# A branch flag one step earlier, a hint for the branch, and the arms in the other order

## The chip, the cores and the metric

The kernel runs on one core of one Trainium2 chip. The metric is the device time in microseconds (us) of one execution. Before the change three runs took 209.24, 209.59 and 210.6 us, median 209.59 us. One more execution was recorded with the hardware profiler; all durations below come from it unless another source is named.

## The reference

The reference mixes two blocks of a model over a sequence of 2048 tokens of width 512, in bfloat16:

```
g = sigmoid((x * gate_w).sum(-1, keepdims=True))
a: q, k, v = x @ wqkv, 32 heads of 16;  pq = q @ w_phi, pk = k @ w_phi (per head)
   phi = concat(softmax(p), softmax(-p)) for p = pq and p = pk
   kv = phi_k^T v;  z = sum of phi_k;  o = (phi_q kv) / (phi_q z + 1e-6);  a = o @ wo
b: z = gelu(x @ w_in) in two halves z1, z2;  z2 = layernorm(z2)
   b = (z1 * (w_sp @ z2 + b_sp)) @ w_out
out = g * a + (1 - g) * b
```

The softmax needs care. `exp` without the row maximum taken off is fast, and it is right as long as no sum of exponentials grows too large. The kernel computes that fast form, keeps watch over the sums, and holds a second, slower form (with the maximum) ready in the same program. A flag computed on the chip decides which of the two delivers the output. With the inputs of the reference the fast form is the one that is used.

## The kernel before

The tokens are cut into 16 tiles of 128 (NT = 16). The first stage computes `z`, the gate and the projections of all tiles. The second computes the keys' features and the products with `w_sp`, in halves of 344 columns (`gg_half`, 32 of them). The last stage is the loop `for j in range(NT)`. Its step j multiplies the queries' features with `kvx` (`q_mm`, L471), divides and gates on VectorE (`q_num`, L477 and L479), transposes `o` into `oT` by a DMA that SyncE issues (L486), and, three steps later, multiplies the finished tile into the output (`out_tile`, L492 and L497; L506 copies the result out of PSUM on ScalarE and L507 starts its DMA). So step 14 runs `out_tile(11)`, step 15 runs `out_tile(12)`, and three output tiles, 13, 14 and 15, are left when the loop ends.

The program is written under a manual schedule: each engine executes its instructions in the order in which the Python code issues them. TensorE (PE in the profile) has the longest list by far, 2746 instructions up to the branch, and its sequencer dispatches them into a queue ahead of their execution.

The flag comes about as follows. GpSimd (POOL) adds up in `worst` all sums and their reciprocals. In step 13 `check_sums` (L455, L456, VectorE, DVE in the profile) turns them into a column of ones and zeros, `safeb`, and `count_safe` (L461) lets TensorE add up that column, into one number in PSUM bank 0: it is 128 if all partitions are safe. In step 14 `copy_count` (L466) copies the number to `flag`. After the loop `nc.values_load` (L614) makes each of the five engines read `flag` into a register of its own. `out_mm` of tile 13 follows, and then the branch (L617): `tc.If(safe < P)`. The first arm is the general form, 1105 TensorE instructions and 319 on VectorE. The `Else` arm is what is executed here. It has 62 TensorE instructions, the copy of tile 13 and all of tiles 14 and 15. In the program's memory the general arm stands right behind the branch and the fast arm behind the general one, so each engine has to jump over the general arm.

```
        if j == NT - 2:
            copy_count()
    safe = nc.values_load(flag[0:1, 0:1], min_val=0, max_val=P)
    out_mm(NT - 3, 5)
```

Tile 15 is split into 384 and 128 columns. The copy of the last 128 columns (L506) and its DMA (L507), both on ScalarE, are the last work of the kernel; the end of the program waits for that DMA.

Of the kernel before, what the change touches and what calls it, by code (L numbers as in the profile page):

```python
# [8 lines left out]
ALU = mybir.AluOpType  # L9
# [5 lines left out]
P = 128  # L15
S = 2048
D = 512
# [5 lines left out]
NT = S // P  # L23
# [17 lines left out]
def kernel(  # L41
# [14 lines left out]
    nc = tc.nc  # L56
# [9 lines left out]
    ps = psp.tile([P, 8, CH], FP32, name="ps")  # L66

    def zbank(t):
# [29 lines left out]
    flag = pers.tile([1, 1], I32, name="flag")  # L98
# [9 lines left out]
        out=ident[:], in_=ident[:], pattern=[[-1, P]],  # L108
# [14 lines left out]
    for d0 in (0, 2):  # L123
# [6 lines left out]
        out=wv[:, :, :],  # L130
        in_=A_wqkv[:, 2 * D:3 * D].rearrange("(dt p) n -> p dt n", p=P),
    )
    for q in range(1, NCH):
        nc.sync.dma_start_transpose(
            out=xT[:, :, q * CH:(q + 1) * CH], in_=x2[q * CH:(q + 1) * CH, :]
        )
        if q == 1:
            nc.sync.dma_start(
                out=wphiW[:, :, :],
                in_=A_w_phi.rearrange("(g h) e f -> (h e) g f", g=NDT),  # L140
# [3 lines left out]
        out=bcolb[:, :, :], in_=B_b_sp.rearrange("(t p) -> t p", p=P)  # L144
# [7 lines left out]
    for t in range(WSLOTS):  # L152
        load_wsp(t)
    nc.sync.dma_start(
        out=w_out[:, 0:NFT - 1, :],
        in_=B_w_out[0:(NFT - 1) * P, :].rearrange("(ft p) n -> p ft n", p=P),
# [4 lines left out]
        out=w_out[0:last_m, NFT - 1, :], in_=B_w_out[(NFT - 1) * P:FH, :]  # L161
    )
    nc.sync.dma_start(
        out=wo[:, :, :], in_=A_wo.rearrange("(g p) n -> p g n", p=P)
# [4 lines left out]
        out=mask16[:], in_=mask16[:], pattern=[[-16, 8]],  # L169
# [3 lines left out]
        out=mask16[:], in_=mask16[:], pattern=[[16, 8]],  # L173
# [210 lines left out]
    def k_proj(t, general=False):  # L384
        ek_t[t] = e_slot(t % 4)
        feat(t, wk, KBANK[t % 2], ek_t[t], general)

    def k_norm(t, watch=True):
        norm(ek_t[t], watch)

    def q_proj(t, general=False):
        eq_t[t] = e_slot(4 + t % 2 if t < 4 else (t - 4) % 6)
        feat(t, wq, QBANK[t % 2], eq_t[t], general)
# [3 lines left out]
    def q_norm(t, watch=True):  # L397
        e = eq_t.pop(t)
        norm(e, watch)
        eT = wqkT[:, 2 * (t % 4):2 * (t % 4) + 2, :].rearrange("p a (b n) -> p (a b) n", n=P)  # L400
        nc.sync.dma_start_transpose(out=eT, in_=e.rearrange("p g a n -> p (g a n)"))
        eT_t[t] = eT
# [10 lines left out]
    def kv_acc(t):  # L413
        for g in range(NHG):
            kv_mm(t, g)

    def kv_extract():
        nc.vector.tensor_tensor(
            out=kvx[:, :, 0:HW].rearrange("p g (h d) -> p g h d", h=4),
            in0=slots[:, :, 0:HW].rearrange("p g (h d) -> p g h d", h=4),  # L420
            in1=mask4[:, None, :, None].to_broadcast([P, NHG, 4, DH]), op=ALU.mult,
        )
        nc.vector.scalar_tensor_tensor(
            out=kvx[:, :, HW:QW], in0=slots[:, :, HW:HW + 1].to_broadcast([P, NHG, 4]),
            scalar=0.5 * DEN_EPS, in1=mask4[:, None, :].to_broadcast([P, NHG, 4]),
            op0=ALU.add, op1=ALU.mult,
        )
# [26 lines left out]
    def check_sums():  # L454
        nc.vector.tensor_reduce(out=worst1[:, 0:1], in_=worst[:], axis=AX.X, op=ALU.max)  # L455
        nc.vector.tensor_scalar(  # L456
            out=safeb[:], in0=worst1[:, 0:1], scalar1=SAFE, scalar2=None, op0=ALU.is_le
        )

    def count_safe():  # L460
        nc.tensor.matmul(  # L461
            ps[0:1, 0, 0:1], lhsT=safeb[:], rhs=ones[:, 0:1], start=True, stop=True
        )

    def copy_count():
        nc.vector.tensor_copy(out=flag[:], in_=ps[0:1, 0, 0:1])  # L466

    oT_t = {}

    def q_mm(t, g):  # L470
        nc.tensor.matmul(  # L471
            slots[:, g, 0:QW], lhsT=eT_t[t][:, g, :], rhs=kvx[:, g, :], start=True, stop=True
        )

    def q_num(t, general=False):
        rd = ring2.tile([P, NHG, 4], FP32, name="rd")
        nc.vector.reciprocal(out=rd[:], in_=slots[:, :, HW:QW])  # L477
        o = ring2.tile([P, D], BF16, name="o")
        nc.vector.scalar_tensor_tensor(  # L479
            out=o[:].rearrange("p (g h d) -> p g h d", g=NHG, h=4),  # L480
            in0=slots[:, :, 0:HW].rearrange("p g (h d) -> p g h d", h=4),
            scalar=gate[:, t:t + 1],
            in1=rd[:, :, :, None].to_broadcast([P, NHG, 4, DH]), op0=ALU.mult, op1=ALU.mult,
        )
        oT = (gTpool if general else oTpool).tile([P, NDT, P], BF16, name="oT")
        nc.sync.dma_start_transpose(out=oT[:, :, :], in_=o[:, :])  # L486
        oT_t[t, general] = oT

    def out_mm(t, b, n0=0, n1=D, general=False):
        uT, oT = uT_t[t], oT_t[t, general]  # L490
        for ft in range(NFT):
            nc.tensor.matmul(  # L492
                ps[:, b, n0:n1], lhsT=uT[:, ft, :], rhs=w_out[:, ft, n0:n1],
                start=(ft == 0), stop=False,
            )
        for g in range(NDT):
            nc.tensor.matmul(  # L497
                ps[:, b, n0:n1], lhsT=oT[:, g, :], rhs=wo[:, g, n0:n1],
                start=False, stop=(g == NDT - 1),
            )  # L500

    def out_copy(t, b, ob, copy, dma, n0=0, n1=D):
        if copy is nc.vector:
            nc.vector.tensor_copy(out=ob[:, n0:n1], in_=ps[:, b, n0:n1])  # L504
        else:
            nc.scalar.activation(out=ob[:, n0:n1], in_=ps[:, b, n0:n1], func=AF.Copy)  # L506
        dma.dma_start(out=out2[t * P:(t + 1) * P, n0:n1], in_=ob[:, n0:n1])  # L507

    def out_buf():
        return ring3.tile([P, D], BF16, name="ob")  # L510

    def out_tile(t, general=False):
        b = (2, 6)[t % 2]
        out_mm(t, b, general=general)
        out_copy(t, b, out_buf(), nc.scalar, nc.scalar)
# [52 lines left out]
    def gg(n, short=()):  # L568
        nonlocal gg_next
        for k in range(n):  # L570
            gg_half(gg_next, short if k == n - 1 else ())
            gg_next += 1
# [21 lines left out]
    for j in range(NT):  # L594
        short = [lambda g=g: q_mm(j, g) for g in range(NHG)]
        if 0 < j and j in gg_at:
            gg(gg_at[j], short)
        else:
            gg(gg_at.get(j, 0))
            for mm in short:  # L600
                mm()
        q_num(j)
        if j + 4 < NT:
            q_proj(j + 4)
        if j + 3 < NT:
            q_norm(j + 3)
        if j >= LAG:
            out_tile(j - LAG)
        if j == NT - 3:
            check_sums()  # L610
            count_safe()
        if j == NT - 2:
            copy_count()
    safe = nc.values_load(flag[0:1, 0:1], min_val=0, max_val=P)  # L614
    out_mm(NT - 3, 5)

    with tc.If(safe < P) as branch:  # L617
        for t in range(NT):
            k_proj(t, general=True)
            k_norm(t, watch=False)  # L620
            kv_acc(t)
        kv_extract()
        for t in range(NT):
            q_proj(t, general=True)
            q_norm(t, watch=False)
            for g in range(NHG):
                q_mm(t, g)
            q_num(t, general=True)
            out_tile(t, general=True)
    with branch.Else():  # L630
        out_copy(NT - 3, 5, out_buf(), nc.vector, nc.sync)
        out_mm(NT - 2, 6)
        out_copy(NT - 2, 6, out_buf(), nc.vector, nc.sync)
        ob = out_buf()
        out_mm(NT - 1, 0, 0, D - P)
        out_copy(NT - 1, 0, ob, nc.vector, nc.sync, 0, D - P)
        out_mm(NT - 1, 1, D - P, D)
        out_copy(NT - 1, 1, ob, nc.scalar, nc.scalar, D - P, D)
# [1 line left out]
_INS = ['A_x', 'A_wqkv', 'A_w_phi', 'A_wo', 'B_x', 'B_w_in', 'B_w_sp', 'B_b_sp', 'B_w_out', 'gate_w']  # L640
_OUTS = [((1, 2048, 512), 'bfloat16')]
# [25 lines left out]
```

## Time and profile before

| what | before |
|---|---|
| median of 3 runs | 209.59 us (209.24 to 210.6) |
| the profiled execution's own time | 209.61 us |
| its span, first to last instruction | 207.9 us |
| TensorE busy | 201.5 us, 97% of the span |
| VectorE, ScalarE, GpSimd busy | 150.9, 80.4, 63.3 us |
| granted TensorE clock | 1.000 over the whole span |

The span is 1.7 us shorter than the time, which also holds what lies around the first and the last instruction. Lines such as L617 are lines of the kernel's file. In the views a sequencer's own records (a register load, a branch, the issue of a DMA) carry a q behind the engine's name; PEld is TensorE's loading of weights, which lies beside its matmuls and has a sequencer in common with them.

### The profile page before, as it was taken

The numbers are of one execution on the slowest core, as the hardware profiler recorded it, in microseconds if no ns is written. First come the engines' busy times: TensorE is split into PE (matmuls) and PEld (weight loads), VectorE is DVE, ScalarE is ACT, GpSimd is POOL, SyncE is SP. The second block draws the span as 40 slices with busy tenths as digits, with TensorE's granted clock in tenths as the row PEclk, the third lists the DMA queues.
The fourth block names the chain that finished last, engine by engine and source line by source line (L and its number), as shares of the span: only waits on it lengthen the run. The fifth ranks groups of instructions, "written<-read, shape, count | busy, mean of one in ns | idle before, by whom it ended". The sixth has DMA issues, their size and how long they took to land.

```text
span 207.9 us, 3748 instructions
## 1 busy us (share of the span) xinstructions
PE 201.5 (97%) x1376; PEld 117.3 (56%) x1400; DVE 150.9 (73%) x310; ACT 80.4 (39%) x142; POOL 63.3 (30%) x79
## 2 busy tenths in 40 slices
PE   8999999999999999999999999999999999999992
PEld 7545554554455666566666667666455554555441
DVE  1049858285978888879797996798988879794521
ACT  3366767666684333341423210222434335321100
POOL 4000000000003555537465673063535353343000
PEclk9999999999999999999999999999999999999999
DMA  6999999994000648463758962335777864967441
GB/s 169 275 168 264 194 195 221 185 223 141 0 3 0 139 79 101 101 143 78 149 103 106 185 129 41 61 78 93 154 151 89 177 140 103 132 139 172 93 87 52
DMA packets 90385, 26.57 MB, mean 128 GB/s; under 512 B 84296, under 2 KB 90360, under 8 KB 90360
## 3 DMA queue, kind: packets, MB, share of 16 engines
q1 hardware_dynamic: 87648, 24.13, 59.7%
q10 hardware_dynamic: 2712, 2.13, 4.0%
q8 instruction: 12, 0.20, 0.4%
q14 instruction: 13, 0.11, 0.2%
HBM read 3.44 MB, written 2.10 MB: 27 GB/s over the span
## 4 chain that ended last, share of the span: by engine, by line
PE 94%; DMA 2%; issue 1%; SPq 0%; DVE 0%; ACT 0%; DVEq 0%
PE ps L435 36%; PE ps L186 18%; PE ps L335 13%; PE ps L492 10%; PE ps L288 7%; PE ps L497 6%; DMA w_in<-in_B_w_in_dram 2%; PE ps L471 2%; PE ps L407 2%; PE ps L311 1%; DVE ob L504 0%; SPq L117 0%; SPq L113 0%; ACT ob L506 0%; DVE w_in L218 0%
## 5 line engine op out<-in xcount | busy, mean ns | idle before, releaser
L435 PE MATMUL ps<-zz,wsp 128*128 128x344 bf16 x512 | 84.1, 309 | 0.1
L367 POOL TENSOR_TENSOR worst<-worst,zr 128x128 f32<-128x128 f32 x32 | 28.6, 894 | 124.5 <-DVE zr L365 110.3
L435 PEld LDWEIGHTS <-wsp 128*128 128x128 bf16 x512 | 49.8, 98 | 27.9
L343 ACT ACTIVATE w_in<-ps 128x512 bf16<-128x512 f32 x56 | 30.1, 596 | 63.4 <-POOL w_in L371 20.8
L186 PE MATMUL ps<-w_in,xT 128*128 128x512 bf16 (+2 forms) x197 | 39.7, 349 | 0.5 <-DVE w_in L218 0.2
L364 DVE TENSOR_REDUCE zr<-w_in 128x64 f32<-128x1024 bf16 x28 | 33.8, 1208 | 0.0
L443 DVE SCALAR_TENSOR_TENSOR u<-ps,bcol,zz 128x344 bf16<-128x344 f32 x32 | 18.4, 574 | 20.4 <-PE ps L471 9.0
L371 POOL TENSOR_TENSOR w_in<-w_in,zr 128x512 bf16<-128x512 bf16 x28 | 29.4, 1050 | 0.0
L186 PEld LDWEIGHTS <-xT 128*128 128x128 bf16 x200 | 18.8, 97 | 18.2 <-issue 0.4
L221 ACT ACTIVATE zz<-ps 128x1376 bf16<-128x1376 f32 (+2 forms) x18 | 21.4, 1190 | 18.5 <-PE ps L186 18.4
L492 PE MATMUL ps<-w_out,uT 128*128 128x512 bf16 (+2 forms) x100 | 23.4, 366 | 0.4
L230 DVE BATCH_NORM_STATS2 stats<-zz 128x6 f32<-128x344 bf16 x32 | 14.8, 506 | 10.9 <-ACT zz L221 10.9
L407 PE MATMUL ps<-vv,w_in 128*128 128x65 bf16 x128 | 21.7, 193 | 0.0
L371 DVE TENSOR_TENSOR w_in<-w_in,zr 128x512 bf16<-128x512 bf16 x28 | 19.4, 692 | 1.0
L506 ACT ACTIVATE ob<-ps 128x512 bf16<-128x512 f32 (+1 forms) x14 | 8.0, 574 | 27.4 <-PE ps L497 18.3
L365 DVE RECIPROCAL zr<-zr 128x64 f32<-128x64 f32 x32 | 17.7, 553 | 1.1
L335 PEld LDWEIGHTS <-xT 128*128 128x128 bf16 x128 | 10.8, 98 | 9.9
L497 PE MATMUL ps<-wo,oT 128*128 128x512 bf16 (+2 forms) x66 | 16.2, 366 | 0.0
L335 PE MATMUL ps<-wk,xT 128*128 128x512 bf16 x57 | 15.7, 379 | 0.3
L335 PE MATMUL ps<-wq,xT 128*128 128x512 bf16 x57 | 15.6, 379 | 0.3
L471 PE MATMUL ps<-kvx,wqkT 128*128 128x68 bf16 x128 | 15.8, 194 | 0.1
L288 PE MATMUL ps<-wv,xT 128*128 128x512 bf16 x61 | 15.5, 379 | 0.2
(64 smaller groups left out, 144.6 us busy)
## 6 DMA issues: line engine op xcount, KB each, us to landing
out_dram<-ob ACTq DMA_DIRECT2D x13, 128.0 KB, 2.7
w_out<-in_B_w_out_dram SPq DMA_DIRECT2D x1, 640.0 KB, 5.7
w_in<-in_B_w_in_dram SPq DMA_DIRECT2D x2, 256.0 KB, 4.2
wv<-in_A_wqkv_dram SPq DMA_DIRECT2D x1, 512.0 KB, 5.2
wo<-in_A_wo_dram SPq DMA_DIRECT2D x1, 512.0 KB, 6.0
w_in<-in_B_w_in_dram SPq DMA_DIRECT2D x1, 352.0 KB, 4.7
w_in<-in_B_w_in_dram ACTq DMA_DIRECT2D x2, 128.0 KB, 4.0
w_in<-in_B_w_in_dram SPq DMA_DIRECT2D x2, 128.0 KB, 3.6
```

Source lines behind the costliest of these rows:

```text
L186: nc.tensor.matmul(zb[:, n0:n1], lhsT=xT[:, dt, t * P:(t + 1) * P], rhs=w_in[:, dt, n0:n1], start=(dt == 0), stop=(dt == NDT - 1),)
L221: nc.scalar.activation(out=zz[:, t, n0:n1], in_=zbank(t)[:, n0:n1], func=AF.Gelu_apprx_tanh)
L288: nc.tensor.matmul(ps[:, b, :], lhsT=xT[:, dt, t * P:(t + 1) * P], rhs=wv[:, dt, :], start=(dt == 0), stop=(dt == NDT - 1),)
L335: nc.tensor.matmul(ps[:, b, :], lhsT=xT[:, dt, t * P:(t + 1) * P], rhs=w[:, dt, :], start=(dt == 0), stop=(dt == NDT - 1),)
L343: nc.scalar.activation(out=e[:, :, a, :], in_=src, func=AF.Exp, scale=sc)
L364: nc.vector.tensor_reduce(out=zs, in_=ev, axis=AX.X, op=ALU.add)
L367: nc.gpsimd.tensor_tensor(out=worst[:], in0=worst[:], in1=zr[:].rearrange("p a h -> p (a h)"), op=ALU.add)
L371: eng.tensor_tensor(out=ev[:, sl, :], in0=ev[:, sl, :], in1=rs[:, sl, None].to_broadcast([P, H, DH]), op=ALU.mult,)
L407: nc.tensor.matmul(slots[:, g, 0:HW + 1], lhsT=ek_t[t][:, g, :, :].rearrange("p a n -> p (a n)"), rhs=vv[:, t, g, 0:HW + 1], start=(t == 0 ...
L435: nc.tensor.matmul(ps[:, b, 0:HF], lhsT=wsp[:, tt % WSLOTS, s, :], rhs=zz[:, s, FH + h * HF:FH + (h + 1) * HF], start=(s == 0), stop=(s == ...
L492: nc.tensor.matmul(ps[:, b, n0:n1], lhsT=uT[:, ft, :], rhs=w_out[:, ft, n0:n1], start=(ft == 0), stop=False,)
L497: nc.tensor.matmul(ps[:, b, n0:n1], lhsT=oT[:, g, :], rhs=wo[:, g, n0:n1], start=False, stop=(g == NDT - 1),)
```

## The change

Four things are changed, all around the branch.

1. `copy_count` becomes `set_flag`: VectorE compares the count with 127.5 and writes 1 to `flag` if some partition is unsafe, else 0. It is called in step 13, directly behind `count_safe`, and no longer in step 14.
2. The five loads of `flag` move into step 14, behind `out_tile(11)`. On TensorE the load is thereby issued 37 instructions earlier, ahead of `q_mm(15)` and `out_tile(12)`; on VectorE ahead of `q_num(15)`; on SyncE ahead of the transposing DMA of `oT(15)`, on ScalarE ahead of the copy of tile 12.
3. Behind its load each engine gets one new instruction, a branch prefetch hint that reads the loaded register and names the branch that comes later. A value of 0 says that the branch is likely taken, that is, that the code at its target will be wanted.
4. The condition is turned round, so that the fast arm is written first. With `preferred_fallthrough_block=False` the `Else` arm, now the general one, is still placed right behind the branch. In the built program the general arm stands first in memory and the fast arm second, as before, and the fast arm is still reached by a taken branch. The instructions of both arms, and what they wait for, are the same but for renumbered semaphore values.

```diff
-    def copy_count():
-        nc.vector.tensor_copy(out=flag[:], in_=ps[0:1, 0, 0:1])
+    def set_flag():
+        nc.vector.tensor_scalar(
+            out=flag[:], in0=ps[0:1, 0, 0:1], scalar1=P - 0.5, scalar2=None, op0=ALU.is_lt
+        )
...
         if j == NT - 3:
             check_sums()
             count_safe()
+            set_flag()
         if j == NT - 2:
-            copy_count()
-    safe = nc.values_load(flag[0:1, 0:1], min_val=0, max_val=P)
+            unsafe = nc.values_load(flag[0:1, 0:1], min_val=0, max_val=1)
+            tc.mark_branch_hint_location("general", unsafe, list(mybir.ALL_ENGINES))
     out_mm(NT - 3, 5)
 
-    with tc.If(safe < P) as branch:
+    with tc.If(unsafe < 1, label="general", preferred_fallthrough_block=False) as branch:
+        out_copy(NT - 3, 5, out_buf(), nc.vector, nc.sync)
+        out_mm(NT - 2, 6)
...
+    with branch.Else():
         for t in range(NT):
             k_proj(t, general=True)
...
-    with branch.Else():
-        out_copy(NT - 3, 5, out_buf(), nc.vector, nc.sync)
-        out_mm(NT - 2, 6)
...
```

## The prediction

> **What bounds the kernel now.** I read the page first: shares of busy time, then the chain that ended last.
>
> ```profile
> PE 201.5 (97%) x1376; PEld 117.3 (56%) x1400; DVE 150.9 (73%) x310; ACT 80.4 (39%) x142; POOL 63.3 (30%) x79
> ...
> PE 94%; DMA 2%; issue 1%; SPq 0%; DVE 0%; ACT 0%; DVEq 0%
> ```
>
> TensorE is the bound, and the chain hardly leaves it. A change around the branch can gain only where TensorE stands still around the branch, so I read the timeline there (start, duration, engine, line; the gap before in brackets).
>
> ```profile
> 196.41 2.07 SPq L486 DMA_TRANSPOSE oT<-o  x1
> ...
> 198.44 1.03 PE L497 MATMUL ps<-wo,oT 128*128 128x512 bf16 x4
> ...
> 199.53 1.04 PEld L492 LDWEIGHTS <-uT 128*128 128x128 bf16 x6 [0.56 <-issue]
> 199.61 1.46 PE L492 MATMUL ps<-w_out,uT 128*128 128x512 bf16 x6
> 199.94 0.69 DVE L504 CAST ob<-ps 128x512 bf16<-128x512 f32 x1 [3.61 <-PE ps L497]
> ```
>
> The four matmuls from 198.44 are the last ahead of the branch, those from 199.61 the first behind it. Matmuls of this shape start 0.216 us apart when nothing is in the way (6 from 199.61 take 1.46 us with the last one's 0.38, so 1.08/5). The last of the four started at 199.09; the next could have started at 199.31 and did so at 199.61. **The branch costs TensorE 0.30 us**, and "issue" says that no data was waited for. The sequencers' own records, by source line, tell why (min/median/max in ns, first start):
>
> ```profile
> L617 POOLq COMPARE_BRANCH  x1: 45/45/45, 195.3 to 195.3; - x1
> L617 PEldq COMPARE_BRANCH  x1: 3932/3932/3932, 195.5 to 195.5; - x1
> ...
> L617 DVEq COMPARE_BRANCH  x1: 72/72/72, 196.5 to 196.5; - x1
> L617 ACTq COMPARE_BRANCH  x1: 54/54/54, 198.9 to 198.9; - x1
> L617 SPq COMPARE_BRANCH  x1: 53/53/53, 199.6 to 199.6; - x1
> ```
>
> The branch is one instruction of 45 to 72 ns on four engines and of 3932 ns on TensorE. In those 3.9 us the DMA records hold one 16384-byte packet of TensorE's instruction queue, from 196.54 to 198.06 us. TensorE fetched the code at the jump's target, and went on 1.4 us after the packet's end. VectorE shows the same: its branch starts at 196.50, an 8192-byte instruction packet runs from 197.54 to 198.09, its next instruction starts at 199.69. ScalarE, GpSimd and SyncE go on 0.47 to 0.53 us after their branches began: their targets were there already.
>
> TensorE hides most of it since its sequencer runs ahead. The branch began at 195.54, when 34 queued instructions had not started; these lasted until 199.31, so 3.77 us of a stall of 3.93 us was covered, and 0.14 us went from its end to the first matmul: 3.93 - 3.77 + 0.14 = 0.30.
>
> **The change part by part.** All terms stand against the profiled execution, 209.61 us with a span of 207.9. The median of the three runs, 209.59, is the same within 0.02.
>
> *The flag, one step earlier.* One 1x1 CAST from PSUM (136 ns) goes, one 1x1 comparison comes; its nearest row is L456, a 128x1 TENSOR_SCALAR of 156 ns. VectorE now waits in step 13 for the count matmul (189.88 to 190.04). Behind it on VectorE stands the L443 that starts at 192.74, after 2.9 us of idle time. Cost 0; without that cover it would be some 0.3 us. `flag` is then ready near 190.3 instead of 194.42.
>
> *The loads, moved.* They last
>
> ```profile
> L614 POOLq TENSOR_LOAD <-flag x1: 824/824/824, 194.5 to 194.5; - x1
> L614 PEldq TENSOR_LOAD <-flag x1: 684/684/684, 194.8 to 194.8; - x1
> L614 DVEq TENSOR_LOAD <-flag x1: 833/833/833, 195.6 to 195.6; - x1
> L614 ACTq TENSOR_LOAD <-flag x1: 477/477/477, 198.3 to 198.3; - x1
> L614 SPq TENSOR_LOAD <-flag x1: 744/744/744, 198.5 to 198.5; - x1
> ```
>
> On TensorE the load was reached at 194.75, when 36 instructions were queued ahead of it. Placed 37 earlier, at the same lead, it falls near 191.8, after the flag. It uses up 0.68 us of a queue that then holds 2.9 us of work (191.8 to 194.73, where `q_mm(15)` begins): cost 0. On VectorE it sits between `q_num(14)` and `q_num(15)`: 193.6 + 0.83 = 194.5, and the L477 behind it starts at 195.19. On ScalarE it follows the DMA issue that ends at 195.90 and ends at 196.4; the next L506 starts at 197.34. On SyncE it now stands ahead of the transposing DMA of `oT(15)`, with the two small L614 records (181 and 28 ns). That DMA was issued at 196.41 and its last landing is at 200.18. From 195.9 on, 0.74 + 0.21 us and the gaps put its issue near 197.2, 0.8 us later, its landing near 201.0. TensorE loads that tile at 202.58, at 202.28 if it gains 0.30: 1.3 us to spare, cost 0.
>
> *The hint.* No row of the trace shows one. From below: its own duration is like that of other sequencer records, 17 to 72 ns, behind a queue of 2.9 us, so nothing; a gain of its own it can't have beyond the 0.30. From above: a hint that holds the sequencer until its packet is there lasts as long as the branch did, 3.93 us. I take the small value, since its operand is a register and nothing behind it needs the fetched code. The packet is then fetched near 193 to 196.7 (same 3.9 us), and the branch, dispatched near 195.5 as before, goes on by 197.2 at the latest (another 0.5 us, as on the three engines whose targets were there). The queue lasts until 199.31. So TensorE's 0.30 us go to 0. What is late next is nothing before the end: tile 14's `oT` lands at 199.14 and is loaded at 200.69.
>
> [...]
>
> *The arms.* In memory they stand as before and the jump is taken as before: 0.
>
> **Sum:** 209.61 - 0.30 = **209.3 us**; the span 207.6. Everything behind the last matmul (its end at 204.12 to 207.90) moves along.
>
> *A term at the end that the change can only brush.* The last output's DMA lands on 15 of 16 engines by 206.07, on the last at 206.88, since an instruction packet of 8192 bytes occupies that engine from 205.44 to 205.98. This costs 0.8 us. One more instruction per engine and an earlier end can move that packet away (0.8 us less, 208.5); the trace doesn't tell whose it is, and it can hardly cost more than it does.
>
> **The rivals.**
>
> *No gain, 209.6.* The hinted code isn't there when the branch comes: TensorE's sequencer crosses into its next block of code between hint and branch, fetches the one after it, as it did all along, and this takes the place of the hinted code. TensorE's packets come every 232 to 274 recorded instructions; from the last one, at 178.9, to the branch there are 238 records. The next crossing is thus due close behind the branch or just before it. If it falls between hint and branch, the stall of 3.93 us stays. For it: that nearness. Against it: before shows no packet between 178.9 and 196.54, where only the target was fetched, and the stream up to the branch grows by one instruction. The same time results if the hint does nothing. 13 in 100. [...] No row of before shows how many blocks TensorE holds.
>
> *The hint holds its engine, 211.1.* TensorE's sequencer then stops for 0.68 + 3.93 = 4.6 us near 191.8. The queue holds 2.9 us of work. TensorE stands still for 1.7 us; the 0.30 us of the branch are gained: 209.61 + 1.7 - 0.3 = 211.0, with dispatch 211.1. It decides from a hint of 2.2 us on (2.9 - 0.68). The same on SyncE would bring `oT(15)` 3 to 4 us later, near 204.5, which TensorE would wait for until then: up to 2.2 us behind 202.28, so at most 211.5. For it: TensorE's branch did hold its sequencer so. Against it: a branch has to have its target before it goes on, a hint has not. 7 in 100.
>
> *The end's packet moves away, 208.5.* As worked out. For it: the packet follows some engine's count of instructions, which grows by one. Against it: what fetches it near the end moves with the end. 20 in 100.
>
> **How the numbers follow.** Forecast 209.3 us, 58 in 100; 208.5, 20; 209.6, 13; 211.1, 7; anything else 2. The range takes in the first three. Above it reaches 0.5 us beyond 209.6, half the way to the highest of the three runs before (210.6), as a median of a few runs can lie off by so much: 208.5 to 210.1 us. What a measurement of this kernel can tell from no change is about 1%, 2.1 us: faster than 207.5 would need about twice the 0.30 and the 0.8 us together, 2 in 100; slower than 211.7 needs the holding hint on TensorE and more behind it, 4 in 100; within 1%: 94 in 100.
>
> **What would show it.** Right: on TensorE a branch record of some 50 ns in place of 3932; its 16384-byte packet near 193 to 195 in place of 196.54; the first L492 behind the branch 0.22 us after the last L497 before it; VectorE's first L504 up to 0.3 us earlier; TENSOR_LOADs near 191 to 196. Wrong: a branch of microseconds again (the hinted code was lost), a gap in TensorE's work between 192 and 195 (the hint holds it), a wait at the L497 of tile 15 (`oT(15)` too late), or a span that moved while TensorE's last matmul didn't, which would be the end's packet and not the branch.

## The result, and the profile after

| | before | after |
|---|---|---|
| median | 209.59 us (209.16 to 210.6, 7 runs) | 208.33 us (208.2 to 208.85, 7 runs) |
| after / before | | 0.9941, 95% interval 0.992 to 0.9962 |
| profiled execution, span | 209.61, 207.9 us | 208.59, 206.8 us |
| last matmul ends | 204.12 us | 203.86 us |
| from there to the end of the span | 3.78 us | 2.97 us |

The change gains 1.26 us, 0.6%. The forecast was 209.3 and the range ended at 208.5: the time lies 0.17 us below it. The last two rows split the 1.06 us of the two profiled spans: 0.26 us came before TensorE's last matmul, 0.81 us behind it.

First the page of after: shares of busy time, VectorE's kind of instruction packets, and the chain.

```profile
PE 201.8 (98%) x1376; PEld 118.3 (57%) x1400; DVE 151.1 (73%) x310; ACT 80.4 (39%) x142; POOL 63.4 (31%) x79
...
q14 instruction: 12, 0.10, 0.2%
...
PE 97%; issue 1%; DVE 0%; ACT 0%; DVEq 0%
```

The same line of the page of before (packets, MB, share of 16 engines):

```profile
q14 instruction: 13, 0.11, 0.2%
```

The work is the same, and one packet of the instruction queue that carries the 8192-byte packets is missing. (The "DMA 2%" that has gone from the chain is something else: by the lines of that chain it was the loading of `w_in` at the start of the kernel, 1.72 to 5.98 us, and it is still there in the kernel with twelve on VectorE below, whose end has no such packet.) Which packet is missing shows in the view of the DMAs from 203 to 207 us. Before (a packet count, MB and share; then the issue of the last output, its size, and the us from issue to its last landing):

```profile
q14 instruction: 1, 0.01, 0.8%
...
out_dram<-ob ACTq DMA_DIRECT2D x1, 32.0 KB, 2.4
```

After, the same view has no instruction packet, and the last output lands 0.8 us sooner:

```profile
out_dram<-ob ACTq DMA_DIRECT2D x1, 32.0 KB, 1.6
```

In the landings themselves, 15 of 16 engines had finished by 206.07 us before and the last one at 206.88; now they finish from 205.62 to 205.82.

The other part is at the branch. The timeline of after (start, duration, engine, line):

```profile
198.50 1.03 PE L499 MATMUL ps<-wo,oT 128*128 128x512 bf16 x4
199.36 1.46 PE L494 MATMUL ps<-w_out,uT 128*128 128x512 bf16 x6
```

Four matmuls at 0.216 us each bring 198.50 to 199.36, so nothing is lost at the branch, where 0.30 us were lost before. (The first matmul behind the branch starts 0.25 us earlier than before, 199.36 against 199.61, and the last one of the kernel ends 0.26 us earlier.) The branch, by engine (min/median/max in ns, first to last start):

```profile
L620 POOLq COMPARE_BRANCH  x1: 65/65/65, 191.0 to 191.0; - x1
L620 PEldq COMPARE_BRANCH  x1: 601/601/601, 195.5 to 195.5; - x1
L620 DVEq COMPARE_BRANCH  x1: 84/84/84, 195.6 to 195.6; - x1
L620 ACTq COMPARE_BRANCH  x1: 68/68/68, 198.4 to 198.4; - x1
L620 SPq COMPARE_BRANCH  x1: 73/73/73, 199.9 to 199.9; - x1
```

And the loads and hints that now precede it on the two engines that had waited for code:

```profile
L616 PEldq TENSOR_LOAD <-flag x1: 489/489/489, 191.9 to 191.9; - x1
L616 DVEq TENSOR_LOAD <-flag x1: 549/549/549, 193.7 to 193.7; - x1
```

```profile
L665 PEldq BRANCH_PREFETCH_HINT  x1: 49/49/49, 192.5 to 192.5; - x1
L665 DVEq BRANCH_PREFETCH_HINT  x1: 55/55/55, 194.3 to 194.3; - x1
```

TensorE's branch takes 601 ns in place of 3932. Its 16384-byte packet runs from 193.73 to 194.66 us, 1.19 us behind the hint, and the branch ends at 196.10, 1.44 us behind the packet. VectorE gained nothing of this kind: no 8192-byte packet follows its hint until 197.05 us, and its next instruction starts at 199.23, 3.58 us after its branch began (3.18 us before). That costs nothing here: ahead of its last copy (203.40 us) VectorE waits 0.93 us for TensorE's matmuls, as before.

### The profile page after: what moved, and what is told of

It reads as the page before. It is cut to its first block, busy times and chain, and to the rows that moved or that the text cites. A ratio compares the mean times of both kernels' runs of the same rounds, so it can differ in the third digit from the quotient of the medians.

```text
span 206.8 us, 3753 instructions
## 1 busy us (share of the span) xinstructions
PE 201.8 (98%) x1376; PEld 118.3 (57%) x1400; DVE 151.1 (73%) x310; ACT 80.4 (39%) x142; POOL 63.4 (31%) x79
## 4 chain that ended last, share of the span: by engine, by line
PE 97%; issue 1%; DVE 0%; ACT 0%; DVEq 0%
PE ps L435 36%; PE ps L186 18%; PE ps L335 13%; PE ps L494 10%; PE ps L288 7%; PE ps L499 6%; PE ps L473 2%; PE ps L407 2%; PE ps L195 2%; PE ps L311 1%; PE ps L201 0%; DVE ob L506 0%; ACT ob L508 0%; PE ps L215 0%; PE ps L461 0%
## 5 line engine op out<-in xcount | busy, mean ns | idle before, releaser
L186 PEld LDWEIGHTS <-xT 128*128 128x128 bf16 x200 | 19.6, 100 | 17.6
L335 PEld LDWEIGHTS <-xT 128*128 128x128 bf16 x128 | 10.8, 98 | 9.9
L499 PE MATMUL ps<-wo,oT 128*128 128x512 bf16 (+2 forms) x66 | 16.2, 366 | 0.0
```

The source lines that it names most:

```text
L186: nc.tensor.matmul(zb[:, n0:n1], lhsT=xT[:, dt, t * P:(t + 1) * P], rhs=w_in[:, dt, n0:n1], start=(dt == 0), stop=(dt == NDT - 1),)
L335: nc.tensor.matmul(ps[:, b, :], lhsT=xT[:, dt, t * P:(t + 1) * P], rhs=w[:, dt, :], start=(dt == 0), stop=(dt == NDT - 1),)
L499: nc.tensor.matmul(ps[:, b, n0:n1], lhsT=oT[:, g, :], rhs=wo[:, g, n0:n1], start=False, stop=(g == NDT - 1),)
```

## The experiments

The branch part came as forecast; the end part came too, which the forecast had left out. Three questions follow. Does the hint, the earlier flag, or something in the layout of the program take away the end's packet? Which of them takes away TensorE's stall? And what is each worth? Three things could decide when a packet comes: the number of instructions that an engine has executed, the place of its code in memory, or the earlier end of the kernel. In the short tables "lost" is the time that TensorE stands still at the branch, "tail" the time from the end of its last matmul to the end of the span, both from the profile of that kernel. Each median stands beside one of the kernel before from the same chip.

### The hint left out, or given to some engines only

The changed kernel without its hint, and with its hint on TensorE alone or on the four others alone:

```diff
-            tc.mark_branch_hint_location("general", unsafe, list(mybir.ALL_ENGINES))
+            # e1: no hint
+            # e2: tc.mark_branch_hint_location("general", unsafe, [PE])
+            # e3: tc.mark_branch_hint_location("general", unsafe, [DVE, Activation, Pool, SP])
```

No hint:

> The changed kernel without its five hints; flag and loads stay early. Two questions. (1) TensorE: if the sequencer's lead of 34 to 36 instructions is what limits the cover, the branch again begins near 195.5, lasts some 3.9 us, and 0.30 us of TensorE are lost between the last L499 before and the first L494 behind it. Rival: if it was the late flag that held the branch back, the branch begins up to 3 us earlier and nothing is lost. (2) The instruction packet of 8192 bytes on the last output's DMA engine (205.44 us in before, 0.8 us of the end). Theory count: it follows the number of instructions of one engine, which is that of before here, so it is back: about 209.6 us. Theory time: it went since flag and loads are early; then it stays away: about 208.65 us with the 0.30 us of TensorE lost.

TensorE alone:

> The changed kernel with the hint on TensorE alone. TensorE loses nothing at the branch (its branch record below 1 us) by either theory. Theory count: the packet at the end belongs to another engine, whose number of instructions is that of before, so it is back: tail behind the last matmul 3.8 us, about 209.3 us. Theory time: the packet stays away, tail 3.0 us, about 208.35 us.

The other four:

> The changed kernel with the hint on the four engines other than TensorE. TensorE's branch lasts 3.9 us again and costs 0.25 to 0.30 us. The packet at the end stays away by theory count and by theory time: tail 3.0 us, about 208.6 us. If the packet were TensorE's doing (theory PE: the hint's fetch on TensorE shifts it), it would be back: about 209.6 us.

| kernel | median (before beside it) | ratio, 95% | TensorE's branch | lost | tail |
|---|---|---|---|---|---|
| no hint | 209.13 (209.45) | 0.999 (0.9978 to 1.0002) | 3749 ns | 0.02 | 3.69 |
| hint on TensorE | 207.94 (209.45) | 0.9933 (0.9917 to 0.995) | 481 ns | 0 | 2.96 |
| hint on the others | 208.23 (209.45) | 0.995 (0.9932 to 0.9968) | 3529 ns | 0 | 2.97 |

The kernel without a hint, branch (by line) and the DMAs at its end:

```profile
L619 PEldq COMPARE_BRANCH  x1: 3749/3749/3749, 195.0 to 195.0; - x1
```

```profile
q14 instruction: 1, 0.01, 0.8%
...
out_dram<-ob ACTq DMA_DIRECT2D x1, 32.0 KB, 2.3
```

The kernel with the hint on TensorE alone, branch:

```profile
L620 PEldq COMPARE_BRANCH  x1: 481/481/481, 194.9 to 194.9; - x1
L620 DVEq COMPARE_BRANCH  x1: 72/72/72, 195.0 to 195.0; - x1
```

Of these three kernels TensorE's branch is short only in the one where TensorE has the hint: 481 ns against 3749 and 3529. But the packet at the end is gone in both kernels with hints, and in the one without it is there, though that one too has its arms in the new order. With the hint on TensorE alone the four other engines execute just as many instructions as without any hint, so a count of executed instructions is not what the packet follows; that theory had expected the packet back, at 209.3 us. And without a hint, with the branch as long as 3749 ns, TensorE loses 0.02 us only, and none with the hint on the others, where some 0.30 us had been expected in both. The interval of the kernel without a hint takes in 1, so its 0.32 us of median are not clear of noise by themselves; the 0.02 us are read from its profile.

### The hint late

The flag and its loads where they were before, the hint directly behind the loads, and the arms in the new order:

```diff
         if j == NT - 2:
-            copy_count()
-    safe = nc.values_load(flag[0:1, 0:1], min_val=0, max_val=P)
+            set_flag()
+    unsafe = nc.values_load(flag[0:1, 0:1], min_val=0, max_val=1)
+    tc.mark_branch_hint_location("general", unsafe, list(mybir.ALL_ENGINES))
```

> Flag, loads and hints at the places of before (flag in step 14, loads behind the loop, the hint directly behind each load, 21 instructions ahead of TensorE's branch). TensorE: hint near 195.5; in the changed kernel the branch went on 3.6 us after the hint, so here at 199.1 plus up to 0.5, against a queue that lasts until 199.31: 0 to 0.3 us lost. Packet at the end: theory count says away (each engine has one instruction more than in before), tail 3.0 us, about 208.4 to 208.65 us; theory time says back, tail 3.8 us, 209.3 to 209.6 us.

Measured 209.0 beside 209.45, ratio 0.9978 (0.996 to 0.9995), tail 2.96 us. Its branch on TensorE, and its timeline there:

```profile
L620 PEldq COMPARE_BRANCH  x1: 4422/4422/4422, 195.2 to 195.2; - x1
```

```profile
197.97 1.03 PE L499 MATMUL ps<-wo,oT 128*128 128x512 bf16 x4
199.77 0.81 PE L494 MATMUL ps<-w_out,uT 128*128 128x512 bf16 x3 [0.77 <-issue]
```

The end's packet is gone here as well, but TensorE loses 0.93 us at the branch (199.77 less 197.97 less four times 0.216), more than without any hint and more than the 0 to 0.3 us expected. The hint came at 195.05, the branch at 195.21 us; the packet started 2.20 us after the hint and 2.05 us after the branch, while in the changed kernel it started 1.19 us after the hint, and without a hint on TensorE 1.0 to 1.15 us after the branch. For the hint the early flag thus buys room ahead of the branch. Why the fetch started late here was not tried.

### Whose packet it is, and what moves it

A hint on one engine alters the built program of the others in one spot. Between the kernel without a hint and one with a hint on GpSimd alone, VectorE's built list differs in a semaphore's number and in one field of the marker at the head of the fast arm, no more. This points to where the code lies. The kernels below leave flag, loads and condition as they were before. They add instructions at the end of the general arm, which is not executed, so that the fast arm behind it starts later in the memory of one engine:

```diff
             out_tile(t, general=True)
+        for _ in range(12):     # ScalarE
+            nc.scalar.activation(out=st[:, 9, 0:1], in_=ones[:, 0:1], func=AF.Copy)
+        for _ in range(n):      # VectorE, n = 12, 128 or 1
+            nc.vector.tensor_copy(out=st[:, 9, 0:1], in_=ones[:, 0:1])
```

Twelve on ScalarE, then twelve on VectorE, which was meant as a control:

> The kernel before, with 12 more ScalarE instructions at the end of the general arm. They are never executed here; they only move ScalarE's fast arm and the end of the program 12 instructions on in memory. Theory place: the packet at the end is ScalarE's, fetched when it enters a new block of 128 instructions 0.56 us before, at its DRAIN behind the fast arm; moved by 12, the arm of 7 and the end of 4 instructions lie in one block, and the packet is gone from the last 2 us: tail behind the last matmul 3.0 instead of 3.8 us, about 208.6 us against 209.45. Theory hint (the packet comes because no instruction of the program is a hint, wherever the code lies): packet and 209.45 us stay. Theory SyncE (the packet is SyncE's, whose records end 0.62 us before it): packet stays too.

> The control: the kernel before, with 12 more VectorE instructions at the end of the general arm, never executed. By theory place nothing moves on ScalarE: the packet at the end stays, tail 3.8 us, 209.45 us within 0.15%. If any change of the layout moves it, it is gone here as well and the time is near 208.6 us.

The hint on GpSimd alone, and the changed kernel again, in the same series:

> The changed kernel with the hint on GpSimd alone, which has no work left at the branch. In its program the marker at the head of the fast arm differs by one flag on all five engines from the one of the kernel without hints. Theory flag (that marker, not the hint's execution, moves the packet, as with the hint on TensorE alone): tail 3.0 us, TensorE's branch 3.5 to 3.9 us, 0 to 0.3 us lost there: 208.2 to 208.5 us. Theory engines (it takes a hint on ScalarE, VectorE or SyncE, or on TensorE): tail 3.8 us, about 209.1 us like the kernel without hints.

> The changed kernel itself, beside the others on one chip: 208.0 to 208.3 us where before takes 209.45 (ratio 0.994), tail 3.0 us, TensorE's branch below 1 us. It says whether the kernel with the hint on TensorE alone (207.94) is any faster than it: if the four other hints cost something, by 0.1 us or more.

Then 128 on VectorE, and one. (TensorE's packets of 16384 bytes come every 232 to 274 recorded instructions in the trace of before; by the same measure, an estimate, 8192 bytes are some 116 to 137. Blocks of 128 instructions, which the expectations assume, lie within that.)

> The kernel before, with 128 instead of 12 VectorE instructions added to the general arm, never executed. [...] Theory place: VectorE's fast arm then stands at the same place within a block as in before, so the packet at the end is back: tail 3.7 to 3.8 us, about 209.5 us, ratio to before 1.000. If any lengthening of VectorE's program takes the packet away, it is gone as with 12: tail 2.95 us, about 208.7 us.

> The same with a single VectorE instruction added to the general arm, as many as the hint adds ahead of VectorE's branch in the changed kernel. Theory edge: in before VectorE's code crosses into a new block exactly behind its last DRAIN; one instruction is then enough to move the crossing ahead of the DRAIN, where VectorE has waited since 199 us, so that its packet comes before the last output's DMA: no packet in the last 2 us, about 208.7 us. If it takes more than one, the packet stays: 209.5 us.

| kernel | median (before beside it) | ratio, 95% | lost | tail |
|---|---|---|---|---|
| 12 on ScalarE | 209.65 (209.57) | 0.9999 (0.9989 to 1.001) | 0.41 | 3.67 |
| 12 on VectorE | 208.75 (209.57) | 0.9958 (0.9943 to 0.9974) | 0.40 | 2.95 |
| hint on GpSimd alone | 208.67 (209.57) | 0.9946 (0.9928 to 0.9963) | 0.16 | 2.96 |
| changed kernel again | 208.44 (209.57) | 0.9951 (0.9935 to 0.9967) | 0 | 2.94 |
| 128 on VectorE | 209.34 (209.41) | 0.9995 (0.9984 to 1.0007) | 0.30 | 3.69 |
| 1 on VectorE | 209.0 (209.41) | 0.998 (0.9967 to 0.9993) | 0.35 | 3.23 |

The kernel with twelve on VectorE, branch, and its last output (no instruction packet in that view):

```profile
L617 PEldq COMPARE_BRANCH  x1: 4052/4052/4052, 195.1 to 195.1; - x1
```

```profile
out_dram<-ob ACTq DMA_DIRECT2D x1, 32.0 KB, 1.5
```

The kernel with 128 on VectorE, the same view of the DMAs:

```profile
q14 instruction: 1, 0.01, 0.6%
...
out_dram<-ob ACTq DMA_DIRECT2D x1, 32.0 KB, 2.3
```

And with one:

```profile
q14 instruction: 1, 0.01, 0.5%
...
out_dram<-ob ACTq DMA_DIRECT2D x1, 32.0 KB, 1.8
```

The control is the finding. Twelve instructions that no engine executes make the kernel 0.82 us faster, with no hint and the flag late; the stall at the branch is as long as in the run beside it on ScalarE. With a whole 128 instructions the packet and the time are those of before. With one, neither of the two outcomes that had been expected came (packet gone, or as before): the packet comes 0.65 us behind the end of the last matmul (204.58 us) in place of 1.32 us, and delays the last output by less. So the packet is a fetch of VectorE's, and the place of its fast arm against blocks of 128 instructions (or of a number that divides 128) decides when it comes: the tail is 2.95 us with twelve, 3.69 with 128 and 3.23 with one.

VectorE's DRAIN behind its last copy points to where it meets the edge of a block. In every kernel here but one this DRAIN starts 0.03 to 0.04 us after the copy has started. In before it runs from 203.69 to 204.26 us, and the packet comes 1.18 us behind it. With one instruction added the DRAIN starts only 0.41 us after the copy, at 203.88 us, and the packet comes 0.69 us after that start: the edge has moved from behind the DRAIN to ahead of it. From the branch on, the DRAIN is VectorE's tenth record, so twelve more instructions ahead of the arm are enough to move the edge out of it. The edge, and this last step with it, is argued; no view shows it.

In all kernels of this document the packet and the tail go together: 3.67 to 3.88 us in the eight with the packet 1.30 to 1.34 us behind the last matmul, 2.94 to 2.97 us in the nine without it, 3.23 us in the one with it at 0.65 us. A hint on TensorE alone, on GpSimd alone or on the four others takes the packet away just as twelve instructions on VectorE do. That the field in the marker shifts VectorE's arm is the likely link, but what the field does was not shown.

### Both parts without a hint

The kernel without a hint and with the early flag, plus the twelve on VectorE; and the hint on TensorE alone once more, since its 207.94 was the lowest of all:

```diff
             unsafe = nc.values_load(flag[0:1, 0:1], min_val=0, max_val=1)
-            tc.mark_branch_hint_location("general", unsafe, list(mybir.ALL_ENGINES))
...
             out_tile(t, general=True)
+        for _ in range(12):
+            nc.vector.tensor_copy(out=st[:, 9, 0:1], in_=ones[:, 0:1])
```

> No hint at all: flag and loads early as in the changed kernel, and 12 unexecuted VectorE instructions added to the general arm. If the change's gain is the sum of the packet at the end (0.82 us by 12 unexecuted instructions in before) and of a shorter stall of TensorE (0.3 us by early flag and loads without hints), this kernel takes about 209.5 - 0.82 - 0.32 = 208.4 us, like the changed kernel (208.33 and 208.44), with a TensorE branch of 3.5 to 3.9 us and 0 to 0.2 us lost there. If the hint itself is worth more than that, it stays 0.2 us or more above 208.4.

> The changed kernel with the hint on TensorE alone, a second time and on another chip. If the four other hints cost something, it is again near 207.95 us (ratio to before 0.9925 to 0.9935); if that was the spread between chips and sessions, 208.2 to 208.4 us (0.994 to 0.995), like the changed kernel.

Measured: 208.31 beside 209.41, ratio 0.9944 (0.9927 to 0.996), lost 0.04, tail 2.97 us; and for the hint on TensorE 208.43 beside 209.41, ratio 0.9954 (0.9939 to 0.9969). The branch without the hint:

```profile
L619 PEldq COMPARE_BRANCH  x1: 3766/3766/3766, 195.4 to 195.4; - x1
```

A kernel with no hint is as fast as the changed one, and the 207.94 does not come again: one hint is not better than five. The parts stand together, as differences in us from the before of their own series: early flag alone -0.32 (not clear of noise by itself), VectorE's arm moved alone -0.82, both -1.10, the changed kernel -1.26 and -1.13.

### Why an early flag shortens the stall without a hint

TensorE's stall has three pieces: from the start of the branch to its packet, the packet, and from the packet's end to the end of the branch. With the flag late they were 1.0 + 1.51 to 1.65 + 1.40 to 1.42 us in before and the four padded kernels, with the flag early and no hint on TensorE 1.11 to 1.15 + 1.01 to 1.33 + 1.41 to 1.50. The packet itself is shorter. The queue also hides a little more: from the start of the branch to the moment when the next matmul could have started (0.216 us after the one before it) it is 3.76 to 3.78 us with the flag late and 3.86 us with it early; with the hint on the four others the whole stall was hidden. Between before and the kernel without a hint 0.18 us come from the shorter branch and 0.11 us from the queue. In before, two other things were looked at that lie beside that packet: the transposing DMA of `oT(15)`, issued 0.86 us after the branch, and GpSimd's own instruction packet. In the early kernels both lie elsewhere. So they were moved away in before, one by one and together, and put back in the early kernel: SyncE got one more load of the flag, which delays its DMA to 1.60 us after the branch; GpSimd got a copy of one column of `o`, which holds it back. That either shares a DMA engine with the packet is the theories' assumption: no view names a packet's engine.

```diff
             copy_count()
+            nc.values_load(flag[0:1, 0:1], engines=[mybir.EngineType.SP], min_val=0, max_val=P)
...
         )
+        if t == NT - 1 and not general:     # NT - 2 in the early kernel
+            nc.gpsimd.tensor_copy(out=st[:, 9, 0:1], in_=o[:, 0:1])
```

SyncE's DMA later:

> The kernel before with one addition: SyncE loads the flag once more into a register, in step 14, ahead of the transposing DMA of oT(15). Nothing else is early and there is no hint. Theory transfer: TensorE's instruction packet at the branch takes 1.5 to 1.65 us where that DMA is issued 0.87 us after the branch began (five kernels), and 1.0 to 1.33 us where it is issued 1.7 to 1.8 us after (four kernels without a hint on TensorE), since they share a DMA engine. Then it is 1.0 to 1.35 us here, TensorE's branch lasts 3.5 to 3.8 us, 0 to 0.1 us are lost there, the packet at the end stays (tail 3.7), and the time is 0.25 to 0.35 us below before (ratio 0.9985). Theory flag (the early flag or TensorE's early load shortens the stall): branch 3.93 to 4.05 us, 0.30 to 0.40 us lost, ratio 1.000.

GpSimd's packet later:

> The kernel before with one 128x1 copy on GpSimd that reads the o of q_num(15), ahead of GpSimd's load of the flag. It holds GpSimd's branch back until o is written, near 196.4 us, so that its own instruction packet (196.62 us in before, beside TensorE's at 196.54) comes near 198.5, behind TensorE's. Theory pool (the two packets share a DMA engine and TensorE's is longer for it): TensorE's packet 1.0 to 1.35 us instead of 1.51 to 1.65, its branch 3.4 to 3.8 us, 0 to 0.1 us lost there, tail 3.7, ratio to before 0.9985. Rival (TensorE's own early load or another engine's shortens it): packet 1.5 to 1.65, 0.30 to 0.40 us lost, ratio 1.000.

GpSimd's branch beside TensorE's again, in the early kernel without a hint:

> The reverse: flag and loads early without hints, as in the run without hints, but with such a copy on GpSimd that reads the o of q_num(14), so that GpSimd loads the flag near 194.5 and branches near 195.3, as in before. Its packet is again beside TensorE's. Theory pool: TensorE's packet 1.5 to 1.65 us, branch 3.9 to 4.05 us, 0.2 to 0.4 us lost, ratio to before 1.000. Rival: packet 1.0 to 1.35 us, 0 to 0.15 us lost, ratio 0.9985 to 0.999 as without the copy.

Both later:

> The kernel before with both additions: SyncE's extra load ahead of the DMA of oT(15), and GpSimd held back until o of q_num(15) is written. Each alone left TensorE's packet at 1.51 to 1.53 us. Theory either (the DMA of oT(15) or GpSimd's packet is enough to lengthen it, so both have to go): packet 1.0 to 1.35 us, TensorE's branch 3.4 to 3.8 us, 0 to 0.1 us lost, packet at the end as before, ratio to before 0.998 to 0.999. Rival (neither matters; it is TensorE's own early load): packet 1.5 us, branch 3.93 us, 0.30 us lost, ratio 1.000.

| kernel | median (before beside it) | ratio, 95% | packet | lost |
|---|---|---|---|---|
| before, SyncE's DMA later | 209.47 (209.52) | 1.0004 (0.9996 to 1.0013) | 1.53 | 0.30 |
| before, GpSimd's packet later | 209.36 (209.57) | 0.9999 (0.9988 to 1.0011) | 1.51 | 0.30 |
| before, both | 209.44 (209.48) | 1.0006 (0.9992 to 1.0019) | 1.53 | 0.55 |
| early flag, no hint, GpSimd back | 209.47 (209.57) | 0.9998 (0.9981 to 1.0015) | 1.62 | 0.46 |

The branches of the last two rows:

```profile
L620 PEldq COMPARE_BRANCH  x1: 4212/4212/4212, 195.1 to 195.1; - x1
```

```profile
L621 PEldq COMPARE_BRANCH  x1: 4185/4185/4185, 195.9 to 195.9; - x1
```

In the early kernel holding GpSimd back brings the long packet back, and by the profile all that the early flag had gained at the branch is lost again (0.46 us in place of 0.02). That is one profiled execution, with 210.32 us among the longest of its twelve runs; the ratios of the two kernels, 0.9998 and 0.999, lie within each other's intervals. In the late kernel neither nor both shorten the packet. So "either is enough" falls, and what else lengthens the packet in before stays open. In the last but one row the extra loss comes from the last piece, 1.69 us in place of 1.42.

## Why the prediction was wrong, point by point

**TensorE's 0.30 us at the branch: right.** The stall was there in every kernel with a late flag (0.30 to 0.93 us), and it is 0 in the changed kernel. The hint costs 44 to 63 ns on its engines and holds none of them, so the rival of 211.1 is out; the hinted code was still there when the branch came, so the rival of 209.6 is out. That a fetch at a crossing would take the place of hinted code was that rival's assumption; no run shows it. The branch record came to 601 ns, not some 50, since TensorE reached it 0.6 us before the hinted code could be used (1.44 us after the packet); the queue covers that. What the forecast did not see is that the early flag alone does nearly the same (0.02 and 0.04 us lost without a hint, 0 and 0.16 us with hints on other engines only). The prediction read the price of a branch from the rows (3932 ns on TensorE), and the runs bear that out: TensorE's lasted 481 to 4422 ns, those of GpSimd, VectorE, ScalarE and SyncE 45 to 84 ns.

**The moved flag and loads at 0: right, the margin was not.** TensorE's load came at 191.94 us (191.8 expected), VectorE's at 193.69 (193.6), ScalarE's at 196.01 (195.9). The DMA of `oT(15)` was issued at 198.02, not 197.2, as SyncE's load took 947 ns and started at 196.47, and its tile landed 4.0 us later, at 202.04; TensorE loaded it at 202.33, so of the 1.3 us to spare 0.29 were left. What became late was the tile before it, `oT(14)`, for which the prediction had 1.5 us to spare (199.14 to 200.69). Its DMA was issued at 195.21 in place of 194.66, its last landing came at 200.44, and TensorE's load waited for it, by the view of TensorE's waits:

```profile
PEld L499 <- DMA oT<-o: 0.2, 1, 0.2
```

That wait of 0.16 us is in the loading of weights (at 200.48 us), and the matmuls do not show it: the first L499 of that tile starts 0.216 us after the matmul before it, at 200.66. So the cost was 0, but with no margin left.

**The step that failed: "Everything behind the last matmul (its end at 204.12 to 207.90) moves along."** It did not: that stretch took 3.78 us before and 2.97 us after. The sum left the packet at the end where it was, at its full 0.8 us, and the 0.81 us that went with it are more than twice the 0.30 us that the forecast was made of. What stands behind this in the prediction is the line on the arms, "In memory they stand as before and the jump is taken as before: 0." The order of the arms is as before, but the order is not all that counts: moving VectorE's fast arm against its blocks, by twelve instructions that are never executed, is worth 0.82 us. That the hint moves it so is likely and not shown; that a hint takes the packet away is shown. In before VectorE's fetch at the end was not hidden: with its packet at 205.44 to 205.98 us the last output took 2.4 us from issue to landing, without it 1.6.

**The rival of 208.5: the right mechanism with the right size, at 20 in 100.** Its reason for the move, an engine's count growing by one, was wrong: with the hint on TensorE alone no other count grows. That it named the size was a reading of the trace, that it named the event was in part luck. Its reason against, "what fetches it near the end moves with the end", holds as long as VectorE's code stays where it is: without the hint the packet came at 204.70 us, 0.74 us earlier than before, with a last matmul that ended 0.75 us earlier, and the tail was 3.69 us. It does not hold once that code is shifted (tail 2.95 us with twelve on VectorE). The packet had a known price and an unknown owner, and the forecast weighed it by a guess on counts and did not ask where the code lies against the fetched blocks. One of the prediction's own signs of being wrong, a span that moves while the last matmul doesn't, pointed there: 0.81 us of the 1.06 us are of that kind.

**The range.** Both parts together were worth 209.61 - 0.30 - 0.81 = 208.50 by the profiled execution, and the range ended right there, with no room below. The profiled execution of the changed kernel took 208.59 us, the median of its seven runs was 208.33, 1.26 us below before. The stall varies from 0.30 to 0.41 us in the unchanged and padded kernels, so 1.1 to 1.2 us are explained, and the rest is within the interval of the ratio (0.8 to 1.7 us).

## What to carry to other kernels

Where the last output of a kernel is a small DMA, look at the instruction packets of its last microseconds: one fetch of 8192 bytes on one of the 16 engines cost 0.8 us here, and a dozen instructions that are never executed removed it. A gain from an edit that also moves code should be tested against such padding before it is credited to the edit. A branch hint needs room: TensorE's took 3.56 us from hint to usable code (192.54 to 196.10 us), and placed 0.16 us ahead of the branch it left the stall longer than no hint (4422 ns). Here it was worth nothing that could be measured beyond the early flag and the moved code: without it, with early flag and padding, the kernel took 208.31 us, with it 208.33 and 208.44.

## What the runs showed of the hardware that was not expected

- Instructions that are never executed changed the time by 0.4% (twelve on VectorE), by nothing (twelve on ScalarE, 128 on VectorE), or by about half of that (one on VectorE).
- A hint on TensorE alone or on GpSimd alone takes the end's packet away from VectorE, which has no hint there (tail 2.96 us in both, 3.69 without any hint).
- VectorE's own hint, at 194.31 us, did not bring its code early: the first 8192-byte packet behind it came at 197.05 us, after the branch at 195.65, and VectorE's next instruction started 3.58 us after that branch began.
- Code was usable only 1.40 to 1.52 us after its packet had ended, in all stalls of TensorE but one (1.69 us).
- The 16384-byte packet of TensorE's branch or hint took 0.93 to 1.65 us, a spread of 0.72 us where the branch of before cost 0.30. GpSimd's packet beside it explains 1.62 in place of 1.18 us in the early kernel; what lengthens it in the late ones is open.
